# Reading the loop count behind the last store, and a new written order of work, in a one-core attention and expert kernel

## The chip, the cores and the metric

The kernel runs on one core of one Trainium2 chip. The metric is device time in microseconds for one execution. The median of three runs of the kernel before is 165.18 us (164.62 to 165.36).

## The reference

There are four batches of 11456 tokens with 128 channels, 32 inducing vectors, and eight experts. First the inducing vectors attend to the tokens, then the tokens attend to the 32 results, and the output goes through the expert that each token's routing picks:

```
h = mab(I, x)                    # per batch: 32 x 128
y = mab(x, h)                    # per token: softmax over 32, then a @ h
logits = norm(y) @ norm(experts).T / tau
e, gate = argmax(logits), softmax(logits)[argmax]
out = gate * (relu(y @ w1[e]) @ w2[e])      # w1 128 x 1024, w2 1024 x 128
```

All numbers are float32. Inputs and outputs are 23.5 MB each.

## The kernel before, in words

Each batch is cut into six blocks of 1920 tokens (the last one padded by 64), 24 blocks in all, numbered 0 to 23. Within a batch the kernel works on the case that one expert wins for all tokens: it then folds the expert into a 32 x 128 table, so that an output block is one small product. A general path stands behind it, a loop over the batches for which this does not hold (L763).

Names of steps, by block unless said otherwise:

- `load`, `loadx`: a block transposed (channels on partitions), and, for the blocks of LOADED, the same block in plain layout. The other blocks are transposed on TensorE (`xt`) and copied out (`xe`).
- `s1`, `e1`, `e1t`, `h`: scores of the inducing vectors, exponentials, a transpose on VectorE, and the sum into `h`. Six of these make one batch.
- per batch, `finish` (L441): `zc`, `hsb`, `rz`, `hd`, `tab`, `vote`, `pick` find the expert; `loadw` reads its number into a SyncE register and loads w1 and w2; `G`, `GT`, `gs`, `gk`, `K`, `Kc`, `K4`, `K4c` fold the expert into the table; `md`, `mdc`, `marg`, `mq`, `mx`, `h2` work out margins for the check.
- `stage2` (L539), for one or two blocks together: `s2`, `am`, `e2`, `ud`, `w`, `n2`, `dt`, `ln`, `ex`, `z`, `fac`, `den`, `lg`, `el`, `S`, `v`, and last the gate `gf`. Then per block `F` (the gate transposed, VectorE), `eg` (exponentials times gate, GpSimd or VectorE), `out` (TensorE), two copies `oe` out of PSUM (ScalarE or VectorE), and `store`. Blocks 15 to 23 do this in two halves, of 8 and 7 groups of 128 tokens: `out 23.0` and `out 23.1`, whose stores are 512 KB and, with the padding cut off, 416 KB.
- `ck1` per batch, then `ck2` to `ck5` (L653), gather the check values over all batches; `verdict` (L663) is seven small VectorE steps that end in `ni`, the number of batches that the general path must do again. It is 0 here.

The order of all 881 steps is written out by hand in ORDER (L42): each engine runs its own steps in that order, and SyncE the loads and stores. AT (L101) says which of the buffers (18 large ones for blocks, 8 PSUM banks and so on) each step takes, and a load into a large buffer waits for all that used the one before. BY_DVE (L110) names the steps that VectorE takes of those that ScalarE or GpSimd would do. FILL (L107) names steps ahead of which TensorE runs some products of zeros (wide ones of 512 columns, narrow ones of 256). A load may be issued only when the load six before it has landed (DEPTH, L125).

Steps are issued inside a block that keeps this order (L696). Behind it stands, at L761, the read of `ni` into a register of all five engines, and at L763 the loop over it:

```
                paced.append(op)
    main.close()


    n_left = nc.values_load(ni, min_val=0, max_val=NB)
    GW = 64
    with tc.For_i(0, n_left, 1) as b:
```

Of the kernel before, what the change touches and what calls it, by code (L numbers as in the profile page):

```python
# [41 lines left out]
ORDER = """load 0.0, xt 0.0, ind, small, load 0.1, s1 0, xt 0.1, m1 0, sha 0, shb 0, xe 0.0, xe 0.1, pz 0, e1 0, load 1, s1 1,  # L42
xt 1.0, xt 1.1, e1 1, e1t 0, load 2, xt 2.1, h 0, s1 2, load 5, en1, xe 1.0, load 3, xe 2.1, xe 1.1, en3, en4,
e1 2, load 4, pad 5, xt 5.1, xt 2.0, xt 5.0, xe 2.0, e1t 1, en5, e1t 2, en6, h 1, s1 3, h 2, loadx 3, py 0, s1 5,
xe 5.0, e1 3, e1t 3, xe 5.1, load 6, pad 11, s1 4, e1 5, e1 4, zc 0, e1t 4, en7, xt 4.0, hde 0, xt 4.1, xe 4.0,
zr 0, h 3, xe 4.1, h 4, rz 0.0, e1t 5, h 5, hsb 0, load 7, rz 0, s1 6, hd 0, m1 6, s1 7, hdc 0, tab 0, s2 0,
tabc 0, vote 0, sha 1, pick 0, shb 1, tabs 0.0, am 0, s2 2, am 2, sta 0, stb 0, s2 1, am 1, s2 4, s2 5, tw 0, e1 7,
e1 6, loadx 7, load 9, load 8, loadx 6, hde 1, oh 0, e2 0, e2 2, e2 1, tabs 0.1, ld 0, tabs 0, loadw 0, s2 3, am 5,
am 3, ud 0, ud 1, e2 5, load 10, ud 2, e1t 6, e2 4, uc 0, e2 3, pz 1, uc 2, w 0, ud 3, w 1, am 4, n2 0, w 2, uc 3,
dt 2, n2 1, e1t 7, w 3, ud 4, load 11, ud 5, s1 9, G 0, ln 0, uc 5, h 6, dt 0, s1 8, n2 3, ex 0, z 0, fac 0, den 0,  # L50
lg 0, el 0, n2 2, ln 2, e1 9, w 4, GT 0, e1 8, h 7, ad 0, n2 4, md 0, xt 10.0, loadx 8, h2 0, ex 2, mdc 0, S 0,
e1t 8, gs 0, xt 9.0, xe 9.0, load 12, zk 0, w 5, v 0, py 1, xe 10.0, xt 11.1, gf 0, pad 17, xe 11.1, hde 2, z 2,
xt 10.1, xt 9.1, xe 10.1, marg 0.0, marg 0.1, gk 0, xt 11.0, load 14, K 0, n2 5, F 1, F 0, ln 4, ex 4, Kc 0, e1t 9,
s1 10, s1 11, xe 9.1, xe 11.0, marg 0, mq 0, mx 0, K4 0, s1 12, K4c 0, dt 4, m1 12, e1 10, h 8, h 9, e1 11, eg 0,
fac 2, den 2, lg 2, sha 2, load 17, el 2, load 13, z 4, fac 4, e1t 10, out 0, shb 2, den 4, S 2, e1t 11, h 10,
eg 1, zc 1, zr 1, e1 12, oe 0.1, ck1 0, loadx 13, loadx 14, h 11, lg 4, v 2, gf 2, rz 1.0, oe 0.0, rz 1, F 2, el 4,
hsb 1, out 1, hd 1, F 3, eg 2, s1 14, hdc 1, load 18, s2 6, oe 1.1, e1 14, s2 8, oe 1.0, S 4, e1t 12, tab 1, v 4,
loadx 15, load 15, tabc 1, s1 13, vote 1, eg 3, am 6, sta 1, stb 1, pick 1, e2 8, tabs 1.0, am 8, gf 4, tabs 1.1,
tabs 1, s2 9, s2 7, e1 13, e2 6, e2 9, loadw 1, tw 1, out 3, am 9, F 4, eg 4, ud 8, ud 9, oe 3.0, load 16, store 0,
xt 12.0, oe 3.1, xt 17.0, w 8, e1t 13, e2 7, xe 12.0, dt 8, z 8, oh 1, am 7, w 9, n2 8, xe 17.0, n2 9, xt 12.1,  # L60
ld 1, ad 1, xe 12.1, ln 8, ex 8, fac 8, pz 2, py 2, out 4, s2 11, den 8, F 5, s2 10, am 11, eg 5, ud 6, w 6,
oe 4.0, oe 4.1, e2 10, e2 11, am 10, out 2, oe 2.1, oe 2.0, G 1, GT 1, gs 1, gk 1, md 1, mdc 1, n2 6, ud 7, uc 7,
dt 6, ud 10, w 10, ud 11, w 7, lg 8, out 5, n2 7, marg 1.0, oe 5.0, h 12, h 13, K 1, marg 1.1, dt 10, w 11,
store 4, ln 6, ex 6, oe 5.1, s1 15, store 1, z 6, fac 6, den 6, lg 6, marg 1, mq 1, el 6, e1 15, el 8, n2 11, Kc 1,
s1 16, K4 1, xt 17.1, xt 18.0, mx 1, e1t 14, K4c 1, e1t 15, S 8, e1 16, s1 17, S 6, v 6, gf 6, store 2, v 8, zk 1,
xe 17.1, gf 8, h 14, e1 17, F 7, s1 18, F 6, e1t 16, loadx 16, xe 18.0, zc 2, h 15, m1 18, zr 2, h 16, load 19,
eg 6, z 10, n2 10, ln 10, ex 10, sha 3, load 20, load 21, out 6, load 23, load 22, e1t 17, rz 2.0, shb 3, F 9,
rz 2, eg 7, fac 10, den 10, lg 10, e1 18, e1t 18, oe 6.1, h 17, hsb 2, ck1 1, F 8, s1 19, oe 6.0, hd 2, xt 18.1,
el 10, e1 19, out 7, hdc 2, S 10, tab 2, xe 18.1, s2 12, tabc 2, vote 2, pick 2, am 12, tabs 2.0, oe 7.0, oe 7.1,
s2 15, s2 13, loadx 22, tw 2, sta 2, stb 2, v 10, eg 8, gf 10, tabs 2.1, tabs 2, s2 14, am 14, e2 12, e2 15, eg 9,  # L70
am 15, loadw 2, s1 20, out 8, loadx 19, e2 13, e2 14, zk 2, ud 14, am 13, ud 15, oe 8.1, e1 20, oe 8.0, ud 12,
uc 14, F 11, ud 13, uc 15, out 9, F 10, eg 11, w 12, dt 14, pz 3, py 3, pad 23, n2 12, e1t 19, w 14, ld 2, ad 2,
eg 10, loadx 20, s2 17, hde 3, s2 16, oe 9.1, w 13, n2 13, dt 12, am 16, md 2, G 2, oh 2, mdc 2, s1 21, e2 17,
oe 9.0, e1 21, GT 2, am 17, gs 2, e2 16, ln 12, ex 12, h 18, h 19, store 6, out 10, w 15, z 14, oe 10.1, oe 10.0,
store 9, z 12, fac 12, marg 2.0, n2 15, den 12, ud 16, n2 14, gk 2, marg 2.1, e1t 20, ud 17, marg 2, w 17, lg 12,
mq 2, el 12, xt 21.0, xe 21.0, ln 14, ex 14, w 16, S 12, n2 16, v 12, fac 14, den 14, xt 21.1, K 2, h 20, s1 22,
lg 14, Kc 2, xe 21.1, n2 17, e1t 21, gf 12, e1 22, el 14, s1 23, xt 23.1, F 13, S 14, mx 2, F 12, e1t 22, eg 13,
xe 23.1, h 21, K4 2, ln 16, K4c 2, dt 16, ex 16, z 16, fac 16, den 16, e1 23, zc 3, xt 23.0, out 11, store 8, v 14,
xe 23.0, e1t 23, zr 3, h 22, h 23, lg 16, el 16, oe 11.1, gf 14, store 10, store 3, store 7, oe 11.0, store 5,
rz 3.0, eg 12, out 12, rz 3, S 16, F 14, F 15.1, store 11, oe 12.1, hsb 3, hd 3, hdc 3, tab 3, tabc 3, F 15.0,  # L80
oe 12.0, v 16, zk 3, gf 16, s2 18, vote 3, am 18, pick 3, sta 3, h2 1, stb 3, tabs 3.0, tabs 3.1, out 13, oe 13.1,
s2 21, eg 14, s2 20, eg 15.0, eg 15.1, tw 3, e2 18, e2 21, store 12, F 17.1, tabs 3, oe 13.0, e2 20, s2 19, e2 19,
out 14, F 16.1, am 21, F 16.0, am 19, ud 18, ud 19, oe 14.0, oe 14.1, am 20, w 18, out 15.0, oe 15.0.1, oe 15.0.0,
ud 20, F 17.0, dt 18, n2 18, uc 20, loadw 3, ud 21, w 19, n2 19, ln 18, ex 18, out 15.1, eg 16.0, eg 16.1, eg 17.0,
z 18, w 20, dt 20, store 13, store 15.0, store 14, s2 22, oe 15.1.1, oe 15.1.0, out 16.1, w 21, eg 17.1, ld 3, G 3,
n2 20, fac 18, e2 22, z 20, n2 21, oe 16.1.1, out 16.0, ln 20, oe 16.1.0, ex 20, oe 16.0.0, am 22, den 18, lg 18,
el 18, fac 20, GT 3, gs 3, gk 3, out 17.0, S 18, den 20, s2 23, oe 16.0.1, oe 17.0.1, K 3, am 23, v 18, oe 17.0.0,
out 17.1, gf 18, Kc 3, F 18.1, lg 20, el 20, store 15.1, S 20, F 18.0, F 19.0, F 19.1, K4 3, eg 18.1, v 20, e2 23,
store 16.1, ud 22, K4c 3, w 22, dt 22, store 16.0, store 17.0, oe 17.1.0, oe 17.1.1, store 17.1, out 18.1, gf 20,
eg 18.0, ud 23, oe 18.1.0, oe 18.1.1, F 21.0, ad 3, out 18.0, eg 19.1, eg 19.0, uc 23, dt 23, oe 18.0.0, oe 18.0.1,  # L90
out 19.0, eg 21.0, z 22, out 21.0, w 23, oh 3, F 21.1, F 20.0, n2 22, oe 19.0.1, oe 19.0.0, oe 21.0.1, ln 22,
oe 21.0.0, h2 2, ex 22, out 19.1, store 18.1, eg 21.1, n2 23, F 20.1, ln 23, oe 19.1.1, fac 22, den 22, md 3,
mdc 3, oe 19.1.0, z 23, store 18.0, lg 22, el 22, ex 23, S 22, eg 20.1, fac 23, den 23, v 22, out 21.1, oe 21.1.1,
store 19.0, oe 21.1.0, store 21.0, gf 22, F 22.1, eg 20.0, lg 23, eg 22.1, out 20.1, oe 20.1.1, oe 20.1.0, h2 3,
out 20.0, store 19.1, store 21.1, el 23, F 22.0, out 22.1, S 23, v 23, ck1 2, ck1 3, eg 22.0, oe 20.0.1, oe 20.0.0,
# [5 lines left out]
AT = """002403102640103267456708042107495a11bc4010020d71e01121345674510fgh10120012335560405107100011301450111210113670  # L101
49d0a20326422601017645110008026110014611460001f0702019a341054121062110153b62115h010g0642031011e4364c0230104051
625010104121640101112004e001h0036764c11010091102146012432g042510560d01342a050111062001110184521012331410621001
# [794 lines left out]
```

## Time and profile before

| | us |
|---|---|
| median of three runs | 165.18 |
| the profiled execution's own time | 166.44 |
| its span, first to last instruction | 164.6 |
| TensorE busy (2113 instructions) | 152.5 |
| VectorE busy (329) | 127.6 |
| ScalarE busy (251) | 112.2 |
| GpSimd busy (187) | 68.3 |
| bytes moved by DMA | 62.33 MB |

Busy time counts the engine's own work alone; register loads, semaphore steps, branches and the issue of DMAs stand under the engine's sequencer (SPq, PEldq and so on) and are not busy time. The profiled execution took 1.26 us longer than the median of the runs, and 1.84 us of it lie outside the span.

### The profile page before, as it was taken

To read this page: it belongs to the slowest core of one execution; us is meant where nothing else is said; L and a number is where in the kernel's file an instruction comes from. 1 tells how busy PE (TensorE), PEld (TensorE's weight loads), DVE (VectorE), ACT (ScalarE), POOL (GpSimd) and SP (SyncE) were. 2 spreads that over 40 slices of the span, in tenths; PEclk is the share of its full clock that TensorE was granted. 3 is DMA by queue.
4 is the path that set the end of the run, shared out by engine and by line. 5 is a ranking of instruction groups with operands and counts; after the bars stand their busy time and mean duration, and the time that the engine had idled before them with its cause. 6 is when DMAs were issued, how large, how long until landed. Compare 5 with 4: busy or idle time off the path is not lost.

```text
span 164.6 us, 5471 instructions
## 1 busy us (share of the span) xinstructions
PE 152.5 (93%) x2113; PEld 82.2 (50%) x2117; DVE 127.6 (78%) x329; ACT 112.2 (68%) x251; POOL 68.3 (42%) x187
## 2 busy tenths in 40 slices
...
GB/s 152 431 423 415 422 418 424 411 420 423 416 412 428 415 417 408 340 411 405 375 420 424 417 279 293 343 424 424 420 398 402 261 424 407 393 327 403 404 301 18
DMA packets 11293, 62.33 MB, mean 379 GB/s; under 512 B 1400, under 2 KB 1408, under 8 KB 11264
## 3 DMA queue, kind: packets, MB, share of 16 engines
...
q8 instruction: 17, 0.28, 0.7%
...
q10 hardware_dynamic: 176, 0.02, 0.1%
...
## 4 chain that ended last, share of the span: by engine, by line
PE 76%; DVE 8%; ACT 4%; POOL 3%; DMA 3%; issue 2%; SPq 0%; POOLq 0%
PE psum L295 60%; PE psum L398 13%; DMA big<-in_xT 3%; PE psum L719 2%; ACT big L292 2%; POOL E2g L624 2%; DVE big L292 1%; DVE am L559 1%; DVE DT L589 1%; DVE n L585 1%; DVE Wp L584 1%; POOL Wp L582 1%; DVE F L622 1%; ACT s L594 1%; ACT gf L611 0%
## 5 line engine op out<-in xcount | busy, mean ns | idle before, releaser
L292 ACT COPY big<-psum 128x960 f32<-128x960 f32 (+4 forms) x73 | 56.1, 800 | 19.9 <-PE psum L398 10.0
L624 POOL TENSOR_TENSOR E2g<-E,F 128x480 f32<-128x480 f32 (+2 forms) x30 | 26.9, 903 | 14.8 <-PE psum L295 8.2
L295 PE MATMUL psum<-E2g,K 32*128 32x480 f32 (+2 forms) x264 | 28.6, 503 | 1.5 <-ACT big L292 0.5
L295 PE MATMUL psum<-big,ind 128*32 128x480 f32 x192 | 25.8, 569 | 0.5 <-DMA big<-in_xT 0.3
L295 PE MATMUL psum<-big,E1T 128*32 128x128 f32 x720 | 24.8, 274 | 0.1
L398 PEld LDWEIGHTS psum<-ident,big 128*128 128x128 f32 x195 | 21.1, 141 | 6.6 <-issue 4.0
L295 PEld LDWEIGHTS psum<-big,E1T 128*32 128x32 f32 x720 | 21.6, 110 | 5.4 <-issue 1.4
L398 PE MATMUL psum<-ident,big 128*128 128x128 f32 x195 | 24.1, 276 | 0.0
L295 PE MATMUL psum<-E,tG 64*64 64x480 f32 x96 | 21.6, 572 | 0.1
L295 PE MATMUL psum<-big,hd 128*32 128x480 f32 x192 | 21.6, 569 | 0.0
L295 PE MATMUL psum<-E,tD 64*64 64x480 f32 x96 | 21.6, 573 | 0.0
L419 ACT ACTIVATE E<-psum,nb 128x480 f32<-128x480 f32 x24 | 15.8, 661 | 7.7 <-PE psum L295 4.6
L428 DVE STREAM_TRANSPOSE E1T<-E 128x480 f32<-128x480 f32 x24 | 15.8, 660 | 5.3 <-ACT E L419 5.2
L292 DVE COPY big<-psum 128x960 f32<-128x960 f32 (+4 forms) x19 | 18.0, 950 | 0.2 <-PE psum L295 0.2
L295 PEld LDWEIGHTS psum<-E2g,K 32*128 32x128 f32 x264 | 10.4, 183 | 14.8 <-issue 3.5
L622 DVE STREAM_TRANSPOSE F<-gf 128x480 f32<-128x480 f32 (+2 forms) x33 | 16.5, 519 | 0.1
L585 DVE TRANSPOSE_TENSOR_REDUCE n<-Wp 128x15 f32<-128x480 f32 x24 | 15.6, 656 | 0.7 <-POOL Wp L582 0.6
L559 DVE TENSOR_REDUCE am<-psum 128x1 f32<-128x480 f32 x24 | 15.1, 643 | 1.1 <-PE psum L295 0.9
L564 ACT ACTIVATE E<-psum,nb 128x480 f32<-128x480 f32 x24 | 14.8, 662 | 0.3
L582 POOL TENSOR_TENSOR Wp<-U,E 128x480 f32<-128x480 f32 x9 | 10.8, 1208 | 9.8 <-DVE n L585 6.7
L295 PEld LDWEIGHTS psum<-E,tG 64*64 64x64 f32 x96 | 6.2, 132 | 12.3 <-issue 6.9
L295 PEld LDWEIGHTS psum<-big,hd 128*32 128x32 f32 x192 | 5.2, 110 | 9.9 <-issue 5.5
...
## 6 DMA issues: line engine op xcount, KB each, us to landing
...
out<-big SPq DMA_DIRECT2D x9, 512.0 KB, 4.6
w<-in_w SPq DMA_DIRECT2D x8, 512.0 KB, 6.1
...
```

Source lines behind the costliest of these rows:

```text
L292: return nc.scalar.copy(out, in_) if e == "ACT" else ENG[e].tensor_copy(out, in_)
L295: return nc.tensor.matmul(out, lhsT=lhsT, rhs=rhs, start=start, stop=stop)
L398: return [nc.tensor.transpose(flat(tp)[:, 128 * (q - q0):128 * (q - q0) + 128], v(q), ident) for q in range(q0, q1)]
L419: return [nc.scalar.activation(ap(e1), ap(ps)[:, :W], AF.Exp, bias=bt.t("nb")[:, 0:1], scale=SCALE, accum_out=bt.t("zk")[:, k:k + 1])]
L428: add(f"e1t {g}", {"DVE": 0.59}, lambda e: [nc.vector.transpose(ap(e1t), ap(e1))], [e1], [e1t])
L559: add(f"am {g}", {"DVE": 0.57}, lambda e, ps=ps, k=k: [v.tensor_reduce(t("am")[:, k:k + 1], ap(ps)[:, :W], AX.X, ALU.max, apply_absolute_v ...
L564: add(f"e2 {g}", {"ACT": 0.56}, lambda e, ps=ps, e2=e2: [nc.scalar.activation(ap(e2), ap(ps)[:, :W], AF.Exp, bias=t("nb")[:, 1:2])], [ps, ...
L582: add(f"w {g}", {"POOL": 1.21}, lambda e, ub=ub, e2=e2, wp=wp: [gp.tensor_tensor(ap(wp), ap(ub), ap(e2), ALU.mult)], [ub, e2], [wp])
L585: add(f"n2 {g}", {"DVE": 0.63}, lambda e, wp=wp, k=k: [v.tensor_reduce(t("n2")[:, k], ap(wp).rearrange("p (q i) -> p q i", i=32), AX.X, AL ...
L622: add(f"F {nm}", {"DVE": 0.09 + 0.51 * part}, lambda e, a=a, f=f, q0=q0, q1=q1: [v.transpose(ap(f).rearrange("p (q i) -> p q i", i=32)[:, ...
L624: add(f"eg {nm}", {"POOL": 0.06 + 1.15 * part, "DVE": 0.2 + 0.54 * part}, lambda e, a=a, f=f, e2=e2, e2g=e2g, c0=c0, c1=c1: [ENG[e].tensor ...
L719: fill = [nc.tensor.matmul(psum[:, s, 0:z.shape[1]], lhsT=z[:, 0:P], rhs=z, start=True, stop=True) for _ in range(n)]
```

## The change

The read of the register moves into the block that keeps the written order, behind its last step. In ORDER the last steps change places: verdict's seven steps stood ahead of `out 23.0` and its copies, and now stand behind the last copies, ahead of `store 23.1`, which becomes the last store. The rest of ORDER, AT, FILL and BY_DVE is replaced by another arrangement of the same 881 steps. The core of the diff (ORDER from the middle of batch 3's last blocks on; AT is left out):

```
-store 20.1, gf 23, F 23.1, store 20.0, oe 22.1.0, oe 22.1.1, out 22.0, eg 23.1, out 23.1, oe 22.0.1, oe 22.0.0,
-store 22.1, store 22.0, F 23.0, marg 3.0, marg 3.1, oe 23.1.1, oe 23.1.0, store 23.1, marg 3, mq 3, eg 23.0, mx 3,
-ck2, ck3, ck4, ck5, verdict.0, verdict.1, verdict.2, verdict.3, verdict.4, verdict.5, verdict, out 23.0, oe 23.0.0,
-oe 23.0.1, store 23.0"""
+marg 3, store 19.1, lg 23, out 22.1, el 23, oe 20.0.1, oe 22.1.0, eg 22.0, mq 3, store 21.1, out 22.0, store 20.1,
+store 20.0, S 23, oe 22.1.1, oe 22.0.0, store 22.1, v 23, mx 3, gf 23, ck2, ck3, ck4, F 23.0, oe 22.0.1,
+store 22.0, ck5, F 23.1, eg 23.0, out 23.0, oe 23.0.0, eg 23.1, oe 23.0.1, store 23.0, out 23.1, oe 23.1.1,
+oe 23.1.0, verdict.0, verdict.1, verdict.2, verdict.3, verdict.4, verdict.5, verdict, store 23.1"""
...
-FILL = """xt 0.0:7:17:n, tab 3:1:2:w, out 17.0:1:1:w, out 19.0:6:1:w, out 19.1:4:1:w, out 21.1:1:4:w, out 20.1:6:1:w,
-out 20.0:0:1:w, out 22.1:6:2:w, out 22.0:2:3:w, out 23.1:6:2:w, ck2:0:3:w, ck4:1:1:w"""
+FILL = """xt 0.0:6:17:n, tab 3:7:2:w, out 19.0:6:1:w, out 19.1:7:2:w, out 21.1:7:3:w, out 20.1:2:2:w, out 20.0:0:1:w,
+out 22.1:4:2:w, out 22.0:0:2:w, ck4:4:1:w, out 23.0:4:4:w"""
...
-    "xe 0.0", "xe 1.0", "xe 2.1", "xe 5.1", "xe 4.0", "tabc 0", "xe 9.0", "K4c 0", "oe 0.0", "eg 2",
-    "gf 4", "xe 12.1", "eg 5", "Kc 1", "gf 8", "oe 6.1", "hdc 2", "tabc 2", "oe 8.1", "eg 11", "Kc 2",
-    "gf 14", "oe 12.1", "tabc 3", "oe 13.0", "oe 17.0.1", "oe 18.0.1", "oe 21.0.0", "oe 19.1.0",
-    "gf 22", "oe 20.1.1", "gf 23", "oe 22.1.1", "oe 23.0.1",)
+    "xe 0.0", "xe 1.1", "xe 1.0", "xe 5.0", "xe 4.0", "hdc 0", "tabc 0", "gf 0", "eg 0", "xe 11.0",
+    "K4c 0", "hsb 1", "gf 4", "oe 4.0", "oe 5.0", "K4c 1", "xe 17.1", "gf 8", "hsb 2", "Kc 2", "gf 14",
+    "oe 12.1", "tabc 3", "oe 13.0", "oe 16.0.0", "Kc 3", "oe 18.0.1", "oe 21.0.1", "eg 20.1",
+    "oe 21.1.0", "gf 22", "oe 20.0.1", "oe 22.1.1", "gf 23", "eg 23.0", "eg 23.1", "oe 23.0.1",
+    "oe 23.1.0",)
...
                 paced.append(op)
+        n_left = nc.values_load(ni, min_val=0, max_val=NB)
     main.close()
-
-
-    n_left = nc.values_load(ni, min_val=0, max_val=NB)
     GW = 64
```

The loads and stores of the new order, which SyncE issues one after the other: load 0.0, 0.1, 1, 2, 5, 3, 4, loadx 3, load 6, 7, loadx 7, load 8, 9, 10, loadx 6, loadw 0, load 11, loadx 8, load 12, 14, loadx 14, load 13, loadx 16, load 15, 17, loadx 13, loadx 15, loadw 1, load 18, 16, store 1, 4, 2, 0, load 19, 20, loadx 20, load 21, 23, loadx 19, loadx 22, loadw 2, load 22, store 6, 8, 9, 10, 5, 3, 7, 11, 12, loadw 3, and then the stores from 14 on. In the order before, from load 16 on: store 0, 4, 1, 2, loadx 16, load 19, 20, 21, 23, 22, loadx 22, loadw 2, loadx 19, loadx 20, store 6, 9, 8, 10, 3, 7, 5, 11, 12, loadw 3, and then the stores from 13 on.

## Rows read from the trace of the kernel before

**Rows 1.** The page: span, and busy us (share of the span) xinstructions.

```profile
span 164.6 us, 5471 instructions
...
PE 152.5 (93%) x2113; PEld 82.2 (50%) x2117; DVE 127.6 (78%) x329; ACT 112.2 (68%) x251; POOL 68.3 (42%) x187
```

**Rows 2.** Table by stretches: busy by engine (x instructions), granted clock, DMA share, GB/s.

```profile
95.00:101.00 6.00, 6.00 (x60) 1.99 (x56) 5.42 (x14) 5.58 (x13) 1.73 (x4) 1.00 0.78 263
...
143.00:147.00 4.00, 3.59 (x47) 1.78 (x45) 3.96 (x11) 3.53 (x9) 3.17 (x6) 1.00 0.78 306
147.00:158.00 11.00, 8.55 (x73) 3.42 (x72) 8.70 (x37) 7.26 (x17) 6.00 (x15) 0.99 1.02 404
158.00:159.00 1.00, 0.00 (x0) 0.00 (x0) 0.00 (x0) 0.00 (x0) 0.00 (x0) 0.50 0.19 73
```

**Rows 3.** The same table, cut where the last gate begins; columns PE, PEld, DVE, ACT, POOL.

```profile
122.00:151.76 29.76, 27.90 (x310) 10.56 (x311) 28.22 (x77) 25.52 (x64) 19.44 (x39) 1.00 0.95 372
151.76:157.73 5.97, 4.39 (x35) 1.62 (x33) 4.64 (x19) 3.16 (x6) 2.10 (x4) 1.00 1.02 404
```

**Rows 4.** Timeline of VectorE from the last gate on: start us, us, what.

```profile
151.76 0.50 DVE L610 RECIPROCAL gf<-v 64x15 f32<-64x15 f32 x2
152.29 0.41 DVE L622 STREAM_TRANSPOSE F<-gf 128x224 f32<-128x224 f32 x1
152.63 0.58 DVE L292 COPY big<-psum 128x448 f32<-128x448 f32 x1
...
153.49 0.38 DVE L531 TENSOR_REDUCE q<-GT 128x8 f32<-128x256 f32 x1
...
154.56 0.17 DVE L536 TENSOR_REDUCE chks<-q 128x1 f32<-128x16 f32 x1 [0.33 <-POOL q L535]
155.15 0.28 DVE L659 TENSOR_REDUCE worst<-psum 24x1 f32<-24x128 f32 x1 [0.43 <-PE psum L658]
155.70 0.19 DVE L661 COPY fl<-psum 1x24 f32<-1x24 f32 x1 [0.27 <-PE psum L660]
155.93 0.16 DVE L668 TENSOR_SCALAR fw<-fl 1x4 f32<-1x4 f32 x1
...
156.96 0.14 DVE L677 CAST ni<-fw 1x1 int32<-1x1 f32 x1
157.03 0.69 DVE L292 COPY big<-psum 128x512 f32<-128x512 f32 x1
```

**Rows 5.** Timeline of TensorE and of ScalarE: last product, copy before the last-but-one store.

```profile
155.59 0.71 PE L295 MATMUL psum<-E2g,K 32*128 32x256 f32 x8
...
154.75 0.54 ACT L292 COPY big<-psum 128x448 f32<-128x448 f32 x1
```

**Rows 6.** SyncE: the read of ni (L761; ns; start), and the last two stores' issues.

```profile
L761 SPq TENSOR_LOAD <-ni x1: 796/796/796, 157.1 to 157.1; - x1
...
155.31 0.33 SPq L637 DMA_DIRECT2D out<-big  x1
...
158.31 0.33 SPq L637 DMA_DIRECT2D out<-big  x1
```

**Rows 7.** Stores of two stretches (KB, us to landing); loop head on SyncE, 158 to 162 us.

```profile
out<-big SPq DMA_DIRECT2D x1, 416.0 KB, 3.5
...
out<-big SPq DMA_DIRECT2D x1, 512.0 KB, 4.7
...
L763 SPq EVENT_SEMAPHORE  x11: 17/28/28, 158.9 to 160.1; - x11
```

**Rows 8.** Groups of VectorE by shape: xcount, busy us, mean ns.

```profile
L624 DVE TENSOR_TENSOR E2g<-E,F 128x480 f32<-128x480 f32 x3 | 1.9, 624 | 0.0
```

**Rows 9.** DMA queues from 158.5 to 164 us: packets, MB, share of 16 engines.

```profile
q14 instruction: 3, 0.02, 1.6%
q8 instruction: 1, 0.02, 1.1%
```

**Rows 10.** Waits of SyncE, 80 to 106 us: us in total, times, longest us.

```profile
SPq L377 <- PE psum L295: 3.7, 1, 3.7
```

More of the change, by code (lines that the diff above doesn't have):

```diff
@@ L39 @@
 LOADED = [3, 6, 7, 8, 13, 14, 15, 16, 19, 20, 22]
[L42 to L95, printed above, removed]
@@ L103 @@
[L103 to L110 removed]
[4 rows of a table removed]
+ORDER = """load 0.0, xt 0.0, ind, small, load 0.1, s1 0, load 1, xt 0.1, load 2, xe 0.1, m1 0, xe 0.0, sha 0, shb 0, e1 0,
@@ new lines @@
+am 1, e1t 7, s2 4, vote 0, pick 0, tabs 0.0, loadx 6, tabs 0.1, tabs 0, s2 2, am 4, e1t 6, e2 2, s2 5, e2 1, s2 3,
+e2 3, e2 4, am 3, loadw 0, ud 0, uc 0, ud 1, ud 2, ud 4, am 2, dt 0, e2 5, ud 5, uc 2, load 11, ud 3, w 1, ld 0,
+w 0, n2 1, n2 0, ln 0, ex 0, ad 0, z 0, hde 1, fac 0, w 2, w 4, loadx 8, s1 8, h 6, h 7, e1 8, load 12, pz 1,
+load 14, s1 9, loadx 14, load 13, loadx 16, G 0, dt 4, den 0, am 5, lg 0, uc 5, uc 3, el 0, n2 4, e1 9, dt 2, md 0,
+e1t 8, n2 2, GT 0, oh 0, xt 9.1, w 5, gs 0, n2 5, w 3, n2 3, ck1 0, xe 9.1, mdc 0, marg 0.0, marg 0.1, load 15,
@@ new lines @@
+load 17, loadx 13, h2 0, xt 9.0, xt 10.1, xe 9.0, xe 10.1, xt 11.1, xt 11.0, xt 10.0, ln 2, xe 11.1, S 0, e1t 9,
+v 0, gf 0, gk 0, F 0, h 8, K 0, py 1, zk 0, z 2, eg 0, s1 11, marg 0, F 1, ln 4, z 4, pad 17, ex 4, fac 4, ex 2,
+Kc 0, fac 2, xe 11.0, den 2, lg 2, eg 1, s1 12, e1 11, s1 10, K4 0, xe 10.0, h 9, m1 12, K4c 0, e1 10, sha 2,
+e1t 11, e1t 10, mq 0, el 2, S 2, mx 0, v 2, out 0, h 10, oe 0.1, gf 2, oe 0.0, zc 1, den 4, zr 1, rz 1.0, shb 2,
+lg 4, h 11, hsb 1, rz 1, el 4, S 4, pz 2, v 4, e1 12, out 1, hd 1, loadx 15, hdc 1, F 2, gf 4, F 3, e1t 12, s1 14,
@@ new lines @@
+s2 6, oe 1.1, s1 13, oe 1.0, am 6, sta 1, stb 1, e1 14, tab 1, tabc 1, s2 8, e2 8, e1 13, vote 1, eg 2, eg 3,
+pick 1, tabs 1.0, tabs 1.1, tabs 1, loadw 1, load 18, s2 9, s2 7, out 3, am 9, am 8, e2 6, e2 9, e2 7, oe 3.1,
+oh 1, oe 3.0, tw 1, ud 8, ud 9, xt 12.0, xe 12.0, xt 12.1, F 5, F 4, am 7, dt 8, w 9, ld 1, w 8, n2 9, eg 4, n2 8,
+ad 1, h2 1, e1t 13, xt 17.0, xe 12.1, out 4, oe 4.0, s2 11, eg 5, oe 4.1, s2 10, am 11, am 10, load 16, xe 17.0,
+out 2, G 1, e2 11, md 1, mdc 1, e2 10, oe 2.1, ud 6, ud 7, ln 8, ex 8, GT 1, gs 1, ud 10, py 2, z 8, fac 8, oe 2.0,
@@ new lines @@
+w 6, gk 1, dt 6, uc 7, ud 11, out 5, w 7, n2 6, marg 1.0, marg 1.1, n2 7, z 6, ln 6, ex 6, fac 6, w 11, den 8,
+lg 8, w 10, marg 1, den 6, h 12, s1 15, dt 10, e1t 14, mq 1, lg 6, oe 5.1, e1 15, el 6, K 1, h 13, s1 18, h 14,
+s1 16, S 6, v 6, gf 6, Kc 1, oe 5.0, el 8, e1 16, store 1, store 4, e1t 15, F 7, store 2, store 0, K4 1, F 6,
+n2 11, xt 18.0, xt 17.1, load 19, m1 18, K4c 1, mx 1, xe 17.1, s1 17, load 20, loadx 20, h 15, n2 10, xe 18.0,
+sha 3, eg 6, z 10, out 6, eg 7, zk 1, e1 17, zc 2, e1t 16, oe 6.0, S 8, e1t 17, shb 3, zr 2, rz 2.0, rz 2, ln 10,
```

42 lines of the change are left out of this document (38 added, 4 removed).

## The prediction, made from these rows

> **What bounds the kernel now.** I read the page first: in a span of 164.6 us TensorE is busy for 93%, VectorE for 78% [rows 1]. The average names no single limit, so I went on by stretches. In that table TensorE is busy without a break from 95 to 101 us, and the DMA engines, full before and after, show a hollow there, a share of 0.78 (1.3 us idle), and another of 0.78 from 143 to 147 (0.9 us idle) [rows 2]. From 147 to 158 us DMA is full again, then it falls to 0.19 at 158 to 159: the stores had run dry before the last one came. From 122 us on VectorE has little room: 28.22 us of 29.76 up to the last gate, and 4.64 of the 5.97 behind it [rows 3].
>
> Then I read the end instruction by instruction. The last gate (gf 23) is two reciprocals that begin at 151.76 and end at 152.26 [rows 4]; call that end G. Behind it VectorE does the two F pieces, a copy out of PSUM (152.63), then four steps on the margins (153.49 to 154.73), ck3 and ck5, the seven verdict steps from 155.93 to the cast into ni at 156.96, and only then the last copy, 157.03 to 157.72 [rows 4]. TensorE's last product, out 23.0, ran from 155.59 to 156.30, so VectorE's half of it was ready 0.7 us before VectorE, busy with the verdict, came to it [rows 4, 5]. SyncE then shows the surprise: the read of ni starts at 157.1 and the last store is issued at 158.31, 0.59 us behind its copy, while the store before went out at 155.31, 0.02 us behind its copy (154.75 + 0.54) [rows 5, 6]. So the register load overtook the store. The store takes 4.7 us to land, at 163.0, all engines wait for it, and the exit to 164.6 takes 1.55 us [rows 1, 7]. SyncE's own steps at the loop head have been over since 160.1 [rows 7].
>
> **The change part by part.**
>
> *Register read behind the store.* It costs nothing new: the same loads on five engines. The store no longer stands behind 0.80 us of load plus its register steps; it goes about 0.1 us after its copy.
>
> *Verdict behind the last copies.* Let T be the end of the last copy. Before: T = 157.72, and the end is T + 6.9. After: the verdict's start to the cast takes 1.03 us; from the cast at 156.96 to SyncE's last step ahead of the landing at 160.1 took 3.1 us, of which the store's issue in the middle was about 0.4, so 2.7. SyncE is through at T + 0.05 + 1.03 + 2.7 = T + 3.8. The store lands at T + 0.1 + its time: 3.5 us for 416 KB while DMA was full, 4.7 for the 512 KB of the last one [rows 7]. The new last store is the 416 KB half, so I take 3.5, T + 3.6. What is late next is therefore the register path by 0.2 us, and the end is T + 3.8 + 1.55 = T + 5.35: 1.5 us less than before at the same T. If the store takes 4.7 it is T + 6.35, and the gain 0.5.
>
> *The last chain.* From G the new order needs on VectorE ck3 0.28, ck5 0.19 and two F pieces of 0.41, then eg 23.0 [rows 4]. An eg on VectorE takes 0.62 us for 480 columns [rows 8], so by estimate 0.35 for 256. That ends at G + 1.65; out 23.0 (0.71) at about G + 2.45, out 23.1 at G + 3.15, its copies at G + 3.8. Before it was G + 5.46. So T comes 1.65 us earlier if G stays. Two covers go with it: before, GpSimd made these products and TensorE stood behind ck4; now ck4 is long done. eg 23.1 (0.35) runs under out 23.0.
>
> *What moves in front of G.* VectorE gets work there: the margin steps and mx (0.95, now ahead of gf 23), the copy oe 22.1.1 and one half copy more (0.58 in each, with five such pieces before G going to six), Kc 3 (0.2, estimate from the small copies) and eg 20.1 (0.35). With oe 22.1.1 counted as that sixth piece it is 2.1 us. VectorE was idle for 1.54 us of the 29.76 before G [rows 3], and not all of it can be filled. If nothing is absorbed, G moves by +2.1 and T by +0.45; if all is, T moves by -1.65. I take the middle, T - 0.6, since GpSimd and ScalarE lose the same pieces and their waits shorten.
>
> *Order before 122 us.* Counting the TensorE operations ahead of the landmarks (hd 0 to hd 3, out 0 to out 14, loadw 1, loadw 2) in both orders, they stand at the same place to within about 3 us of work, and no load or copy is added or taken away. VectorE loses two full eg and one full copy and gains a gate and small copies; the totals agree to half a microsecond. I take 0 and bound it by the two hollows in DMA: at best both filled, though only some of that reaches the end, -1.0; at worst one more of their size, +1.0.
>
> *SyncE's queue.* The loads that stood behind loadw 2 (loadx 19, loadx 20) now stand ahead of it, load 22 goes behind; loadx 16 moves from behind the first stores to ahead of them, and store 0 to behind stores 1, 4, 2. The number of transfers ahead of loadw 2 is 41 in both. Nothing, while DMA has its backlog.
>
> *Fills.* 20 wide ones for 22, and the same 17 narrow ones. They lie in waits of TensorE for GpSimd and VectorE. Nothing, if the clock holds.
>
> **Sum.** -1.5 (end behind T) - 0.6 (T) + 0 (before) = -2.1 us on the profiled execution, span 164.6 to 162.5, its own time 166.44 to 164.3. The median of the runs is 165.18, 1.26 below that execution; the difference carries over: **163.1 us**. Ends: all absorbed gives -3.15, and an order that fills some of the hollows up to -1.0 more, but DMA was full to 158 with 0.5 MB left, so it can't all come; about 161.4. No absorption (+0.45) and a landing as slow as the old one (-0.5) cancel to nothing, 165.1, a corner of two bad ends; one of them alone gives 164.1.
>
> **Rivals.**
>
> *The loop's branch becomes the end and slows down.* In the end stretch the profile shows three instruction transfers (0.02 MB; 1.6% of 16 engines over 5.5 us, 1.4 us in all) and a longer one of the same size in all (1.1%, 0.97 us) [rows 9], beside a single store. SyncE's loop head then ran under the landing; now it is the last thing by 0.2 us. If such a transfer holds the branch up for its full 0.97 us behind the last two stores, the end is T + 6.3 and the time 164.1. For it: the margin is thin. Against it: by then both stores are mostly out. Chance 0.13. The Trainium skill, "Runtime: NRT & Kernel Launch", Instruction fetch mechanics, says that a taken branch out of the loaded window must wait for a DMA of its target; the trace has such transfers, and does not show which engine waited for one.
>
> *No change.* TensorE's clock reads 0.99 up to 158 and 0.50 from 158 to 159, behind the last matmul at 156.3 [rows 2, 5]; with three fills ahead of ck2 gone it could fall before the last outs. Half clock doubles out 23.0 and out 23.1, +1.4: 164.5. Or the change doesn't do what it says, and the register load still stands ahead of the store: then verdict (1.1) and load (0.8, and 0.3 of steps) delay it to T + 2.3, it lands at T + 5.8, end T + 7.35: 165.1. For: it happened before. Against: the read is now inside the block whose order is kept. Chance 0.12 together.
>
> *Slower: SyncE starves DMA ahead of loadw 2.* By the slots, load 21, load 23, loadx 19 and loadx 22 now wait for buffers that h 15, h 16, h 17 and s2 12 free; before, only load 22, loadx 22 and the two behind loadw 2 waited like that. SyncE waited 3.7 us for TensorE at one such load, and DMA was at 0.78 there [rows 2, 10]. Each load is 960 KB, some 2.3 us of DMA. If the backlog ends at load 21 instead of at loadw 2, DMA is short by two more loads, 4.6 us, of which TensorE's wait for batch 3's data passes 3.5 on: 163.1 + 3.5 = 166.6. It decides only when the hollow grows by over 3 us, since the end gives 2.1 back. Against: six loads may be in flight, some 14 us of DMA, and 41 transfers stand ahead as before. Chance 0.09.
>
> **How the numbers follow.** The likeliest case has 0.66. A measurement of this kernel tells about 0.5%, 0.83 us, from no change: faster is under 164.35, slower over 166.0. Likeliest (0.65 of its 0.66) and the branch (0.12 of 0.13) fall on faster: 0.77; same 0.14 with the no-change case and the two rests; slower 0.09. The range from 161.4 to 164.8 holds the likeliest, the branch and the half clock, and leaves out the starved queue and half of the rest.
>
> **What would show it.** The register load on SyncE starts behind the last store, and that store 0.1 us behind its copy; the seven verdict steps follow the last copy; that copy ends at about 157.1 in the span; the store lands some 3.5 us after its issue and is no longer waited for long; DMA has no hollow ahead of its last store. Wrong if G comes later than about 154.4, if DMA's hollow around 95 us grows, or if the end behind the last copy is over 6 us.

## The result, and the profile after

The changed kernel takes 163.12 us, median of 4 runs (162.94 to 163.18); the kernel before took 165.27 us beside it (164.62 to 166.2). The ratio is 0.9864, 95% interval 0.9815 to 0.9913: 1.4% faster, with the whole interval below 1, and 2.15 us between the medians. (The ratios leave disturbed runs out, so they need not be the quotient of the medians shown.) The profiled execution took 162.94 us, its span 161.1 instead of 164.6 us [rows 1].

The page of the changed kernel, as [rows 1]:

```profile
span 161.1 us, 5470 instructions
...
PE 151.1 (94%) x2112; PEld 82.2 (51%) x2115; DVE 129.2 (80%) x334; ACT 111.8 (69%) x246; POOL 69.9 (43%) x186
```

The totals say little. VectorE does 1.6 us more than before, and the kernel is faster nevertheless. The tables by stretches tell where that work went. Columns: PE, PEld, DVE, ACT, POOL, granted clock, DMA share, GB/s. After, cut at the end of the last gate (152.13) and of the last copy (155.68), and below it the stretches of [rows 2]:

```profile
0.00:122.00 122.00, 120.25 (x1786) 70.71 (x1788) 96.61 (x240) 84.51 (x181) 49.55 (x145) 1.00 0.99 399
122.00:152.13 30.13, 28.48 (x310) 10.30 (x311) 28.81 (x81) 25.44 (x63) 20.30 (x41) 1.00 0.95 375
152.13:155.68 3.55, 2.40 (x22) 1.16 (x21) 2.90 (x9) 1.89 (x4) 0.00 (x0) 1.00 0.90 364
...
95.00:101.00 6.00, 6.00 (x60) 1.88 (x52) 4.80 (x11) 5.90 (x13) 2.37 (x6) 1.00 0.98 370
...
155.00:156.00 1.00, 0.00 (x0) 0.00 (x0) 0.97 (x5) 0.48 (x2) 0.00 (x0) 1.00 0.34 135
156.00:159.00 3.00, 0.00 (x0) 0.00 (x0) 0.63 (x5) 0.00 (x0) 0.00 (x0) 0.87 0.80 321
```

Before, cut at the same two events (152.26 and 157.72):

```profile
0.00:122.00 122.00, 120.18 (x1773) 70.06 (x1773) 94.69 (x235) 83.57 (x182) 46.79 (x146) 1.00 0.99 394
122.00:152.26 30.26, 28.40 (x312) 10.66 (x312) 28.71 (x78) 26.01 (x65) 19.94 (x39) 1.00 0.95 373
152.26:157.72 5.46, 3.89 (x33) 1.53 (x32) 4.15 (x17) 2.67 (x6) 1.60 (x4) 1.00 1.02 405
```

Read the third number behind the comma, VectorE. Up to 122 us it has been busy for 96.61 us instead of 94.69, 1.92 us more. From there to the last gate it does as much as before (28.81 and 28.71), though the margin steps and a half copy have been added there, and the gate ends at the same place (0.13 us earlier). So as much work has left this stretch as has come in. Behind the gate the stretch falls from 5.46 to 3.55 us. These two events are called G (end of the last gate) and T (end of the last copy), as in the prediction: T comes 2.04 us earlier, at 155.68.

What paid for the added steps shows at the gate ahead of the last one (gf 22) and at the check steps of batch 2 (ck1 2). VectorE before, then after:

```profile
149.23 0.50 DVE L610 RECIPROCAL gf<-v 64x15 f32<-64x15 f32 x2
...
151.22 0.15 DVE L646 TENSOR_REDUCE chks<-am 128x1 f32<-128x6 f32 x1
```

```profile
118.09 0.15 DVE L647 TENSOR_REDUCE chks<-am 128x1 f32<-128x6 f32 x1
...
148.15 0.50 DVE L611 RECIPROCAL gf<-v 64x15 f32<-64x15 f32 x2
```

From gf 22 to G it takes 3.48 us now and took 2.53 before, so that stretch, with the margin steps in it now, is longer by 0.95 us. But gf 22 ends at 148.65 instead of 149.73, and ck1 2 has moved from behind it to 118.09. The new order is ahead before the last stretch begins, and spends that lead there.

The end, instruction by instruction: VectorE after, as [rows 4].

```profile
151.62 0.51 DVE L611 RECIPROCAL gf<-v 64x15 f32<-64x15 f32 x2
152.11 0.28 DVE L660 TENSOR_REDUCE worst<-psum 24x1 f32<-24x128 f32 x1
...
152.85 0.39 DVE L623 STREAM_TRANSPOSE F<-gf 128x224 f32<-128x224 f32 x1
153.17 0.67 DVE L625 TENSOR_TENSOR E2g<-E,F 128x256 f32<-128x256 f32 x2
154.46 1.22 DVE L293 COPY big<-psum 128x512 f32<-128x512 f32 x2 [0.62 <-PE psum L296]
155.60 0.15 DVE L669 TENSOR_SCALAR fw<-fl 1x4 f32<-1x4 f32 x1
...
156.62 0.14 DVE L678 CAST ni<-fw 1x1 int32<-1x1 f32 x1
```

No margin step and no verdict step is left between gate and copies. VectorE now waits 0.62 us for TensorE, where before the product waited for VectorE. The verdict's first step begins as the last copy ends (155.60, 0.08 us before that copy's end in the profile), and the cast is over at 156.76.

SyncE after, as [rows 6]: the last two stores, the register load (ns; first and last start), and SyncE's steps at the loop head ahead of its wait for that landing.

```profile
155.22 0.33 SPq L638 DMA_DIRECT2D out<-big  x1
...
155.75 0.33 SPq L638 DMA_DIRECT2D out<-big  x1
```

```profile
L759 SPq TENSOR_LOAD <-ni x1: 869/869/869, 156.8 to 156.8; - x1
...
L762 SPq EVENT_SEMAPHORE  x11: 17/27/28, 158.2 to 159.4; - x11
```

The last store goes 0.07 us behind its copy (0.59 before) and the load stands 1.05 us behind the store. What ends last has changed too. The store of 416 KB lands 3.35 us after its issue, at 159.10, as the view of the transfers has it for 155.7 to 159.2 us (queue: transfers, MB, share of 16 engines; store: KB, us to landing):

```profile
q14 instruction: 1, 0.01, 0.9%
...
out<-big SPq DMA_DIRECT2D x1, 416.0 KB, 3.4
```

SyncE is through with the last of its eleven steps ahead of the wait at 159.39, 0.29 us later, so no one waits for the landing any more. The exit takes 1.7 us from there (1.5 from the landing before).

### The profile page after: what moved, and what is told of

It is laid out like the page before. It is cut to its first block, busy times and chain, and to the rows that moved or that the text cites. A ratio compares the mean times of both kernels' runs of the same rounds, so it can differ in the third digit from the quotient of the medians.

```text
span 161.1 us, 5470 instructions
## 1 busy us (share of the span) xinstructions
PE 151.1 (94%) x2112; PEld 82.2 (51%) x2115; DVE 129.2 (80%) x334; ACT 111.8 (69%) x246; POOL 69.9 (43%) x186
## 4 chain that ended last, share of the span: by engine, by line
PE 79%; DVE 8%; ACT 4%; DMA 3%; issue 1%; POOL 1%; SPq 0%; POOLq 0%
PE psum L296 64%; PE psum L399 14%; DMA big<-in_xT 3%; DVE big L293 2%; ACT big L293 2%; DVE F L623 2%; PE psum L720 1%; DVE v L607 1%; ACT E L565 1%; DVE DT L590 1%; DVE gf L611 1%; ACT s L595 1%; POOL lg L603 1%; ACT E L420 0%; POOL E2g L625 0%
## 5 line engine op out<-in xcount | busy, mean ns | idle before, releaser
L625 POOL TENSOR_TENSOR E2g<-E,F 128x480 f32<-128x480 f32 (+2 forms) x29 | 27.3, 947 | 14.1 <-DVE F L623 6.6
L296 PE MATMUL psum<-big,ind 128*32 128x480 f32 x192 | 25.1, 570 | 0.2 <-DMA big<-in_xT 0.2
L296 PE MATMUL psum<-big,hd 128*32 128x480 f32 x192 | 22.4, 570 | 0.0
L293 DVE COPY big<-psum 128x512 f32<-128x512 f32 (+4 forms) x19 | 17.7, 936 | 0.7 <-PE psum L296 0.6
L603 POOL TENSOR_TENSOR lg<-DT,den 128x240 f32<-128x240 f32 (+1 forms) x13 | 8.0, 614 | 5.3 <-DVE den L601 5.0
## 6 DMA issues: line engine op xcount, KB each, us to landing
big<-in_xT SPq DMA_DIRECT2D x4, 928.0 KB, 10.4
```

Of the source, the lines that this page charges most:

```text
L293: return nc.scalar.copy(out, in_) if e == "ACT" else ENG[e].tensor_copy(out, in_)
L296: return nc.tensor.matmul(out, lhsT=lhsT, rhs=rhs, start=start, stop=stop)
L603: add("lg " + nm, {"POOL": 0.64}, lambda e: [gp.tensor_tensor(u("lg"), dv(), u("den").rearrange("p a q -> p q a").unsqueeze(3).broadcast_t ...
L625: add(f"eg {nm}", {"POOL": 0.06 + 1.15 * part, "DVE": 0.2 + 0.54 * part}, lambda e, a=a, f=f, e2=e2, e2g=e2g, c0=c0, c1=c1: [ENG[e].tensor ...
```

## The experiments

All compare with the kernel before by ratio (median of their own runs in brackets). G, T, last issue and landing are from the profiled execution, us in the span.

| kernel | G | T | G to T | last store issued | lands after | span | median (runs) | ratio, 95% interval |
|---|---|---|---|---|---|---|---|---|
| before | 152.26 | 157.73 | 5.47 | 158.31 | 4.74 | 164.6 | 165.27 (4) | |
| e9_before | 152.56 | 158.03 | 5.47 | 158.33 | 4.3 | 164.2 | 165.2 (10) | 1.0014, 0.9978 to 1.005 |
| e1_reg | 152.72 | 158.19 | 5.47 | 158.25 | 3.36 | 163.1 | 164.15 (10) | 0.9913, 0.9883 to 0.9943 |
| e2_tail | 151.89 | 156.68 | 4.79 | 156.74 | 4.17 | 162.4 | 164.2 (9) | 0.9916, 0.9881 to 0.9952 |
| e4_order | 152.38 | 156.68 | 4.30 | 156.75 | 4.73 | 163.1 | 164.84 (12) | 0.9981, 0.9952 to 1.001 |
| e12_lead | 152.43 | 157.10 | 4.67 | 157.16 | 4.15 | 162.8 | 164.89 (10) | 0.9979, 0.9938 to 1.0019 |
| after | 152.13 | 155.68 | 3.55 | 155.75 | 3.35 | 161.1 | 163.12 (4) | 0.9864, 0.9815 to 0.9913 |
| e10_after | 151.88 | 155.44 | 3.56 | 155.50 | 3.33 | 160.8 | 162.88 (4) | 0.985, 0.9772 to 0.9929 |
| e6_regout | 152.3 | 155.87 | 3.57 | 155.93 | 3.96 | 161.5 | 163.1 (4) | 0.9864, 0.9811 to 0.9917 |
| e7_pool | 152.38 | 156.07 | 3.69 | 156.13 | 3.21 | 161.1 | 163.08 (4) | 0.9862, 0.9806 to 0.9918 |
| e8_nofill | 152.21 | 155.77 | 3.56 | 155.83 | 3.29 | 161.1 | 163.21 (4) | 0.988, 0.9825 to 0.9935 |
| e5_gap | 152.29 | 155.84 | 3.55 | 155.91 | 3.31 | 160.8 | 162.74 (6) | 0.9844, 0.9804 to 0.9884 |
| e11_gap | 152.74 | 156.31 | 3.57 | 156.37 | 3.34 | 161.3 | 162.53 (4) | 0.9825, 0.9747 to 0.9903 |

Note first how far G moves without any change. The kernel before has 152.26 and 152.56, and e1_reg and e2_tail, whose work up to G is the same, have 152.72 and 151.89. A single G or T is thus good to some 0.8 us only; the distance G to T repeats within 0.02. From G to the end of the span it is 12.3 and 11.6 us in the two profiles of before, 10.4 in e1_reg, 10.5 in e2_tail, 10.7 in e4_order, 10.4 in e12_lead, and 9.0 and 8.9 in the changed kernel.

**e1_reg: the read alone, in the order before.**

```
+        n_left = nc.values_load(ni, min_val=0, max_val=NB)
     main.close()
-
-
-    n_left = nc.values_load(ni, min_val=0, max_val=NB)
```

> The kernel before, with the read of ni alone moved behind the last store. Theory (the end is the later of the store's landing and SyncE's loop head, plus 1.5 us): the last store is issued 0.1 us behind its copy instead of 0.6, at about 157.8 us of the span, so it lands 0.5 us earlier, and the loop head, at 160.1, stays hidden: 0.5 us faster, 164.7. Rival (the landing of the profiled execution was held up by an instruction transfer, which comes a fixed time after the branch): the store's last packets are out before that transfer, and the landing comes up to 1.8 us earlier than in that one profile, but only 0.5 earlier in the median. Rival (the read costs nothing where it stood, the store waits for DMA anyway): no change, 165.2.

Register load of SyncE and of ScalarE, and the last store's landing:

```profile
L758 ACTq TENSOR_LOAD <-ni x1: 531/531/531, 157.6 to 157.6; - x1
...
L758 SPq TENSOR_LOAD <-ni x1: 281/281/281, 158.6 to 158.6; - x1
```

```profile
out<-big SPq DMA_DIRECT2D x1, 512.0 KB, 3.4
```

ScalarE still reads at 157.6, but SyncE, whose own order now holds the store first, reads at 158.6. The store goes 0.06 us behind T instead of 0.59 (0.30 in e9_before, where the load took 0.52 us and not 0.80), and the time falls by 0.87%, over half of the whole change's 1.36%. G to T is untouched. The gain, 1.4 us by the ratio, is over twice the 0.5 us that was expected, so the store's earlier issue explains less than half of it. What else differs in the profiles is the landing: the same 512 KB store lands after 3.36 us here and after 4.74 before (4.3 in e9_before). Why is open; it is taken up in the last section.

**e2_tail: the read and the place of the verdict, the rest of the order as before.**

```
-ck2, ck3, ck4, ck5, verdict.0, ..., verdict, out 23.0, oe 23.0.0,
-oe 23.0.1, store 23.0"""
+ck2, ck3, ck4, ck5, out 23.0, oe 23.0.0,
+oe 23.0.1, verdict.0, ..., verdict, store 23.0"""
```

> The kernel before, order and assignment kept, with the verdict behind the last copies and the read of ni behind the last store: the two tail edits without the rest. Theory: the last copy ends 0.65 us earlier (157.05 of the span), SyncE is through 3.8 us later, the end is 5.35 us behind the copy: span 162.4 instead of 164.6. If the profile of before was typical of its runs, the median falls by as much, to 163.0, and the rest of the change is worth nothing; if that profile had a landing 1.3 us later than the median run has, the median falls by 0.9 to 164.3 and the new order is worth the other 1.2. Rival (the 512 KB store, still the last one here, takes 4.7 us to land whatever is around it): end 6.35 us behind the copy, span 163.4.

VectorE's last copy, and the transfers behind the last issue (156.7 to 161 us):

```profile
155.99 0.69 DVE L292 COPY big<-psum 128x512 f32<-128x512 f32 x1 [0.47 <-PE psum L295]
```

```profile
q8 instruction: 1, 0.02, 1.4%
...
out<-big SPq DMA_DIRECT2D x1, 512.0 KB, 4.2
```

G to T falls by 0.68: the copy no longer waits for the seven steps, but, as its bracket says, for TensorE. The time is e1_reg's all the same. In the profiles the landing, 4.17 us after the issue and 0.81 later than e1_reg's, sets the end and takes the gain back; 15 of the store's 16 parts were there after 2.82 us.

**e4_order: the new order alone**, with the read outside the block and the verdict ahead of the last products again.

```
-store 22.0, ck5, F 23.1, eg 23.0, out 23.0, ..., oe 23.1.0, verdict.0, ..., verdict, store 23.1"""
+store 22.0, ck5, F 23.1, eg 23.0, verdict.0, ..., verdict, out 23.0, ..., oe 23.1.0, store 23.1"""
...
-        n_left = nc.values_load(ni, min_val=0, max_val=NB)
     main.close()
+    n_left = nc.values_load(ni, min_val=0, max_val=NB)
```

> The kernel after with both tail edits undone: the verdict ahead of the last products (between eg 23.0 and out 23.0, so eg 23.1 and out 23.1 wait 1.1 us for it) and the read of ni outside the ordered block. Theory: the last gate comes where it came in the kernel after (152.1), the last copy 1.0 us later (156.7), the store lands 3.4 us behind it and the end is 5.0 us behind the copy: 0.6 us slower than after, 163.7. Rival (the new order is worth nothing, the tail edits all): 165.2. Rival (the tail edits are worth nothing): 163.1.

VectorE's cast and last copy; SyncE's load; the last store:

```profile
154.75 0.14 DVE L678 CAST ni<-fw 1x1 int32<-1x1 f32 x1
...
156.06 0.62 DVE L293 COPY big<-psum 128x448 f32<-128x448 f32 x1 [0.27 <-PE psum L296]
```

```profile
L762 SPq TENSOR_LOAD <-ni x1: 599/599/599, 154.9 to 154.9; - x1
```

```profile
q8 instruction: 1, 0.02, 1.3%
...
out<-big SPq DMA_DIRECT2D x1, 416.0 KB, 4.7
```

The load is through long before the last copy and delays no store. G to T falls by 1.17 against before, but the time by 0.19%, which can't be told from nothing (the interval holds 1). 163.7 was expected, and 164.84 is nearer to the rival by which the new order alone is worth nothing. Again the landing, 4.73 us for 416 KB, ends last: 156.75 + 4.73 and 1.6 us of exit are the span of 163.1. In G to T the parts add up: 0.68 (e2_tail) and 1.17 make 1.85, and the whole change has 1.92. In the time 0.84 (the read included) and 0.19 make 1.03% against the whole's 1.36%, and the intervals are too wide to say whether these differ.

**e6_regout: the changed kernel with the read outside the block again** (e1_reg's edit, backwards).

> The kernel after with the read of ni outside the ordered block again, all else kept. Theory: the read goes ahead of a store only because ni was ready before that store's copy; with the verdict behind the last copies it stands behind the last store in any case, so nothing changes: 163.1, and SyncE's end looks the same. Rival (outside the block it overtakes the last store): the store is issued 2.2 us later and the end comes 2 us later, 165.1.

```profile
L762 SPq TENSOR_LOAD <-ni x1: 284/284/284, 157.4 to 157.4; - x1
```

SyncE's load stands 1.5 us behind the last issue (155.93) without being told to: the verdict ends after the last store is out. The ratio, 0.9864, is that of the changed kernel. So the read's move is worth 0.87% in the order before, and nothing once the verdict is behind the copies: the two edits cure the same fault.

**e7_pool: the changed kernel with eg 23.0 and eg 23.1 on GpSimd.**

```
-    "oe 21.1.0", "gf 22", "oe 20.0.1", "oe 22.1.1", "gf 23", "eg 23.0", "eg 23.1", "oe 23.0.1",
+    "oe 21.1.0", "gf 22", "oe 20.0.1", "oe 22.1.1", "gf 23", "oe 23.0.1",
```

> The kernel after with eg 23.0 and eg 23.1 given back to GpSimd. Theory: each takes 0.73 and 0.66 us there instead of 0.35, and a hand-over between engines of 0.1 us each way is added; the first one starts earlier, behind its own F: out 23.0 comes 0.2 to 0.4 us later and out 23.1 0.5 later, the last copy 0.5 us later, the end 0.5 us later, 163.6. Rival (TensorE's fills and the copies before hide it): 163.1.

GpSimd's two products, and TensorE's last ones:

```profile
153.29 1.34 POOL L625 TENSOR_TENSOR E2g<-E,F 128x256 f32<-128x256 f32 x2 [1.68 <-DVE fl L662]
```

```profile
154.07 1.28 PE L296 MATMUL psum<-E2g,K 32*128 32x256 f32 x16 [0.22 <-POOL E2g L625]
```

The pair takes twice as long (1.34 us, 0.67 on VectorE), but VectorE is free meanwhile, and TensorE had four fills in that place anyway. G to T grows by 0.14 only and the time is the same, not 0.5 us longer as expected. Which of the two engines makes these products does not matter here.

**e8_nofill: the changed kernel without the five fills ahead of ck4 and out 23.0.**

```
-... out 22.0:0:2:w, ck4:4:1:w, out 23.0:4:4:w"""
+... out 22.0:0:2:w"""
```

> The kernel after without the five fills ahead of ck4 and out 23.0 (products of zeros). Theory: the granted clock stays at full, since the wait it leaves is only 1.1 us; out 23.0 starts up to 0.1 us earlier: 163.0 to 163.1. Rival (the clock falls to half before the last products): out 23.0 and out 23.1 take 1.4 us longer together, 164.5, and the clock column shows 0.5 there.

TensorE's last products, and the stretch around them (columns as above):

```profile
153.77 1.09 PE L296 MATMUL psum<-E2g,K 32*128 32x256 f32 x16 [1.06 <-DVE E2g L625]
```

```profile
152.50:154.80 2.30, 1.21 (x17) 0.85 (x17) 1.68 (x6) 0.84 (x3) 0.00 (x0) 1.00 1.00 403
```

TensorE stands idle for 1.06 us ahead of out 23.0 and the granted clock stays 1.00 (the 2.4 GHz level); the 16 products take the same 1.09 us as with the fills. The fills here earn nothing, and the clock did not fall before the last products in this execution even without them.

**e12_lead: e2_tail, and the margins and mx moved ahead of the last gate, eg 23.0 and 23.1 on VectorE**, but the order before 122 us as it was. It asks whether the lead is needed.

```
-store 22.1, store 22.0, F 23.0, marg 3.0, marg 3.1, oe 23.1.1, oe 23.1.0, store 23.1, marg 3, mq 3, eg 23.0, mx 3,
+..., store 22.1,
+store 22.0, F 23.0, oe 23.1.1, oe 23.1.0, store 23.1, eg 23.0, ...
...
-    "gf 22", "oe 20.1.1", "gf 23", "oe 22.1.1", "oe 23.0.1",)
+    "gf 22", "oe 20.1.1", "gf 23", "eg 23.1", "eg 23.0", "oe 22.1.1", "oe 23.0.1",)
```

The four margin steps now stand behind h2 3, and mx 3 ahead of gf 23.

> The two tail edits on the order before, and in addition two of the new order's moves at the end alone: the four margin steps and mx go ahead of gf 23, and VectorE takes eg 23.1 and eg 23.0. Theory (the new order could put that work ahead of the gate only because VectorE had done 1.9 us more by 122 us; here it has no such lead): gf 23 ends 0.7 to 0.95 us later than in the run with the tail edits alone (151.9 there), the last copy comes 4.0 us behind it instead of 4.8, so it ends where it did, 156.7 to 156.9, and the median stays at 164.2. Rival (VectorE's idle time takes the moved work in): the gate stays at 151.9 to 152.3, the last copy ends at 156.0, 0.7 us faster, 163.5.

The table up to 122 us of e12_lead, then VectorE's step ck3 and TensorE's ck2 in it:

```profile
0.00:122.00 122.00, 120.73 (x1781) 70.55 (x1781) 95.02 (x236) 83.62 (x182) 46.90 (x147) 1.00 0.99 397
```

```profile
155.29 0.28 DVE L661 TENSOR_REDUCE worst<-psum 24x1 f32<-24x128 f32 x1 [0.80 <-PE psum L660]
...
153.73 0.66 PE L297 MATMUL psum<-E2g,K 32*128 32x224 f32 x8
154.32 0.82 PE L721 MATMUL psum<-zwide 128*128 128x512 bf16 x3
154.98 0.27 PE L660 MATMUL psum<-ident,chks 128*24 128x128 f32 x1
```

The gate moved back (by 0.54 us, 0.7 to 0.95 expected), but the last copy (157.10 against 156.7 to 156.9) and the median (164.89 against 164.2) are misses. VectorE has no lead (95.02 us done by 122, e2_tail 94.92), and the moved steps (0.95 us) push the gate back: from gf 22's end to gf 23's it takes 3.23 us instead of e2_tail's 2.52, and G comes 0.54 later. Behind the gate the chain shortens by 0.12 only, since in TensorE's order the reduction of the checks (154.98) stands behind out 23.1 and three fills, and VectorE waits 0.80 us for it. In the changed kernel the stretch from gf 22 to gf 23 is longer too (3.48), but there gf 22 comes earlier: over all profiles it ends at 148.40 to 149.27 us with the new order and at 149.20 to 150.19 with the old one (149.20 here). All kernels with the new order had 96.06 to 96.89 us of VectorE's work done by 122 us, all with the old one 94.20 to 95.02. Part of the difference is not a lead: the new BY_DVE also gives VectorE other steps before 122 us (gf 0 and two hsb copies, for instance) and takes some away. Which moves of the new order make it was not tried apart.

**e5_gap, and e11_gap as its repetition: three verdict steps in VectorE's wait for out 23.0.**

```
-..., eg 23.1, oe 23.0.1, ..., oe 23.1.0, verdict.0, ..., verdict, store 23.1"""
+..., eg 23.1, verdict.0, verdict.1, verdict.2, oe 23.0.1, ..., oe 23.1.0, verdict.3, ..., verdict, store 23.1"""
```

> The kernel after, with the first three verdict steps put into VectorE's wait of 0.62 us for out 23.0. Theory: the loop head sets the end and the landing comes 0.3 us before it would be waited for: SyncE is through 0.44 us earlier, the landing takes over, and the end comes 0.3 us earlier, 162.8. Rival (the landing sets the end already): no change, 163.1. Rival (the steps overrun the wait and push the copies): 0.1 to 0.2 us slower.

> The kernel after with the first three verdict steps in VectorE's wait for out 23.0, once more, beside the kernel after. Theory: 0.3 to 0.4 us below it, 162.7 to 162.8, with the landing and the loop head ending within 0.3 us of each other. Rival: no difference on the same chip.

VectorE in e5_gap, and SyncE's loop head:

```profile
153.94 0.15 DVE L669 TENSOR_SCALAR fw<-fl 1x4 f32<-1x4 f32 x1
...
154.62 1.22 DVE L293 COPY big<-psum 128x512 f32<-128x512 f32 x2 [0.28 <-PE psum L296]
155.76 0.16 DVE L674 TENSOR_TENSOR fl<-fl,limit 1x24 f32<-1x24 f32 x1
...
156.33 0.14 DVE L678 CAST ni<-fw 1x1 int32<-1x1 f32 x1
```

```profile
L762 SPq EVENT_SEMAPHORE  x11: 17/28/28, 157.8 to 159.0; - x11
```

The steps fill 0.34 us of the 0.62 us of wait, and G to T stays 3.55. The cast ends 0.63 us behind T instead of 1.08. The loop head is through at 159.0, and now the landing (155.91 + 3.31 = 159.22) is last again, so 0.2 us of the 0.45 is lost. Medians are 0.38 and 0.35 us under the changed kernel's of the first comparison and of its own repetition. By its median it is the fastest version in both, though the intervals overlap and one of e11_gap's four runs (163.19) is slower than all of e10_after's.

**e9_before and e10_after: both kernels unchanged, once more.**

> The kernel before once more, unchanged. Theory: the profiled execution shown was 1.3 us longer than the median because its last store landed late, its last part 1.3 us behind the other fifteen, behind a 16 KB instruction transfer; in another profile the landing comes 3.4 us behind the issue instead of 4.7, and the span is 163.2. Rival (the execution was longer elsewhere, spread over its length): the landing takes 4.7 us again and the gates come earlier.

> The kernel after, unchanged, once more beside the next one. Theory: the loop head sets the end, the landing is hidden up to 3.7 us behind the store's issue: 163.1, and the runs lie within 0.7 us of each other, against 1.5 us and more for kernels whose last store's landing sets the end.

Transfers of e9_before behind its last issue (158.3 to 162.7 us):

```profile
q8 instruction: 1, 0.02, 2.2%
...
out<-big SPq DMA_DIRECT2D x1, 512.0 KB, 4.3
```

They repeat: 1.0014 and 0.985. The landing of e9_before, 4.3 us, is nearer to the 4.7 of the first profile than to the 3.4 expected, so a late landing is not peculiar to that one execution. The ten runs of the kernel before lie between 164.48 and 166.21; the four after between 162.69 and 163.0.

## Why the prediction was right, and where it was not

The median, 163.12 us, is the predicted 163.1. The mechanism at the end of the kernel held. That the number is exact is luck: two errors of 1.4 us cancel.

**Right: the end behind T.** Forecast T + 5.35, measured 161.06 - 155.68 = 5.38. The store goes 0.07 us behind its copy (forecast 0.1), lands 3.35 us after its issue (3.5), SyncE is through at T + 3.71 (3.8), the exit takes 1.67 (1.55), and the register path is the later of the two, by 0.29 us (0.2). That the moved read no longer overtakes the store is shown by e1_reg, and e6_regout adds what the prediction lacked: moving the verdict would have done it alone.

**Right, a little too dear: the last chain.** Forecast G to T 3.8, measured 3.55. GpSimd could have kept the two products (e7_pool).

**Wrong: "What moves in front of G", "I take the middle, T - 0.6".** T moved by -2.04, beyond the end of -1.65 that stood for full absorption. The added steps were sized well: 2.1 us forecast, and VectorE is busy for 96.61 + 28.81 instead of 94.69 + 28.71 us up to G, 2.02 more (a net of all that the new assignment moves). The step that failed is the room for them. I listed what comes into the stretch from 122 us to the gate, set it against that stretch's 1.54 us of idle time, and did not ask what leaves it; the order before 122 us I put at 0. But check steps (ck1 2, h2 1 and h2 2) and the start of a copy of 960 columns, which lay behind 122 us, now lie before it, in a part where VectorE had been idle for 122 - 94.69 = 27.3 us, and gf 22 comes 1.08 us earlier. That such a lead is needed is borne out by e12_lead: without it the margins ahead of the gate lengthened the way from gf 22 to G by 0.71 us, and nothing in that order pays for it. How the order before 122 us makes the lead stays open. The sum of the terms is then -1.65 (chain) - 0.25 (chain shorter than forecast) - 0.13 (G, within its spread) = -2.03.

**Wrong: "the difference carries over".** The profiled execution of before was 1.26 us above its median, the one after 0.18 below. So the spans differ by 3.5 us and the medians by 2.15. The kernel before spreads from 164.48 to 166.21 (e9_before), and its profiled execution (166.44) lay above all ten, with a late landing; in after the loop head hides landings up to 3.6 us behind the issue. The forecast for the profiled execution was 164.3, measured 162.94. The 1.4 us by which T came earlier than forecast and the 1.4 us by which the distance to the median shrank offset each other.

**The rivals.** SyncE's loop head is the last thing, as the branch rival wanted, but from the cast's end to the wait it took 156.76 to 159.39, 2.6 us, no longer than before (157.10 to 160.1, with the store's issue of 0.4 in it). No change by a fall of the clock: refuted by the granted clock of 1.00 from 152.13 to 155.68 us, and it stayed there in e8_nofill. No change by a load that still overtakes: refuted by the rows of SyncE. SyncE starving DMA ahead of loadw 2: from 95 to 101 us DMA is at 0.98 instead of 0.78 (0.89 in e9_before, so that hollow is not the same in every execution), and G did not move later. One sign of the prediction did not hold: DMA does have a hollow ahead of the last store, 0.34 from 155 to 156 us. The stores run dry before the last one comes, as they did before.
